# An SSD scan feeding a bilinear FFN: the first input halves, the weight transfers and the order of the first three pairs are rearranged

## The chip, the core and the metric

One core of a Trainium2 chip runs the kernel. Its five engines have queues of their own: TensorE (PE, with weight loads shown as PEld), VectorE (DVE), ScalarE (ACT), GpSimd (POOL) and SyncE (SP, which issues DMAs here and computes nothing). The metric is the device time of one execution in microseconds (us); lower is better.

## The reference

A selective state-space scan gives y; y, laid out as 3072 tokens by 256 features, goes through a bilinear feed-forward. Per batch b (4) and head h (8), over 768 positions, with a state of 16 by 32:

```python
cum = np.cumsum(la, axis=-1)                    # la = log a, within a chunk
L = np.exp(cum[:, :, :, None] - cum[:, :, None, :]) * causal
M = np.einsum('bhin,bhjn->bhij', Cc, Bc) * L
y = einsum(M, xc) + einsum(Cc, state) * exp(cum)
state = decay_full * state + sum_j(Bc xc decay_from_j)
...
a = x @ w_a; b = x @ w_b                        # x: y as 3072 x 256, d_ff = 1536
return (a * b @ w_out).astype(np.float32)
```

The chunk length is free in exact arithmetic; the kernel uses 128.

## The kernel before, in words

The sequence is cut into 6 blocks of 128 positions, and the batches into 2 couples; a *pair* p is one block of one couple (p = 2 * block + couple), so there are 12, each with 256 tokens. Rows of a pair's tiles are 64 partitions for one batch (bt = 0) and 64 for the other, two positions to a partition (index r).

For a pair the work is:

- six loads (load, L127; load1, L119): halves bt = 0, 1 of B, C and x, 64 KB each for B and C and 128 KB for x;
- scale_bc (L235) multiplies B and C by decay factors fB and fC into bm and cm, scale_x (L226) makes a 16-bit X16 of x; mostly on POOL;
- transposes (L252): four on PE, then ACT makes two copies bt and one copy ct;
- scores (L270): 32 small matmuls into the PSUM tiles SC0 and SC1;
- mask (L303), four per pair: DVE multiplies a PSUM bank by the causal mask into T1; or, "by_pool", ACT copies the bank to tmp and POOL multiplies;
- pv (L347): matmuls of the carried state (Sbd) with C and of T1 with X16, ds_mm for the state update, then ACT evacuates X2T, the transposed y; state (L380) updates the state on DVE and POOL;
- six units (unit, L409): each forms 256 of the 1536 hidden features: 8 matmuls with Wa and Wb into two PSUM banks, an ACT copy asb of the first, and a DVE product hk with the second;
- two out_half (L455): 12 matmuls of hk with Wo, an ACT copy osb and a store on SP.

The pool psf has four PSUM banks handed out in turn to the two banks of each unit, the one of each out_half, and the temporaries fps, tb, tc, py, gps. A bank is free again when its reader (asb, hk, osb, a copy) is done.

Decay factors: scan (L190) forms cumulative products Pr of a on DVE, sel_over_mid (L194) selr, and factors_mm (L203) matmuls of the two in fp32 give fC and, by a reciprocal, fB. This is done for block 0 first (8 matmuls) and for blocks 1 to 5 later (40 matmuls). hr, hs, hsx and a small matmul gps (which read the constant c32) give the decays G of the state.

The order on every engine is written out by hand: the program runs under a manual schedule, and each engine takes its instructions in the order of the source. From pair 4 on a loop (L592) repeats one pattern. Pairs 0 to 3 have a sequence of their own (L475 to L590), since the pipeline has to be filled: pair 0 is done in two halves (pv_u and evac0, u = 0, 1) so that its first unit starts early, with matmuls of zeros (warmup, L183) put between, whose results nobody reads.

DMAs are issued from three queues. SP: a, then halves of B, x, B, C, B, x, x of pairs 0 and 1, c32, then load(2), load(3) and so on. ACT: both halves of pair 0's C, half its x, half of pair 1's C. POOL: the constant ch, and the weights, which are converted to 16 bits on the way: load_w (L169) moves a third of Wa and a third of Wb (256 KB each as stored); thirds 0 and 1 early, third 2 (L498) after POOL's scaling of pair 1, then Wo (L499, 768 KB).

Of the kernel before, what the change touches and what calls it, by code (L numbers as in the profile page):

```python
# [22 lines left out]
def kernel(  # L23
# [13 lines left out]
    nc = tc.nc  # L37
# [75 lines left out]
    def tiles(p):  # L113
        Bn = inp.tile([128, H, 2, N], f32, name="bn", tag="bn")
        Cn = inp.tile([128, H, 2, N], f32, name="cn", tag="cn")
        Xn = inp.tile([128, H, 2, D], f32, name="xn", tag="xn")
        pair_in[p] = (Bn, Cn, Xn)

    def load1(eng, p, which, bt):  # L119
        blk, bp = divmod(p, NBP)  # L120
        src = (B, C, x)[which][2 * bp + bt, :, blk * Q : (blk + 1) * Q, :]
        return eng.dma_start(  # L122
            pair_in[p][which][64 * bt : 64 * bt + 64].rearrange("i h r n -> i h (r n)"),
            src.rearrange("h (i r) n -> i h (r n)", r=2),
        )

    def load(p, eng=None):  # L127
        tiles(p)
        return [load1(eng or nc.sync, p, w, bt) for w in range(3) for bt in range(2)]

    nc.sync.dma_start(a_sb, a.rearrange("b h (k q) -> (b h) k q", q=Q))
    tiles(0)
    tiles(1)
    load1(nc.scalar, 0, 1, 1)
    load1(nc.sync, 0, 0, 0)
    load1(nc.scalar, 0, 1, 0)
    load1(nc.sync, 0, 0, 1)
    nc.scalar.preload_act_table_set("natural_log_exp_and_others")
    load1(nc.scalar, 0, 2, 1)
    load1(nc.sync, 0, 2, 0)  # L140
    load1(nc.scalar, 1, 1, 1)
    load1(nc.sync, 1, 0, 0)
# [1 line left out]
    load1(nc.sync, 1, 0, 1)  # L144
    load1(nc.sync, 1, 2, 0)
    load1(nc.sync, 1, 2, 1)
    nc.sync.dma_start(c32, p32_t.ap())
    load(2)
    nc.vector.memset(warm.bitcast(u32), 0)
    nc.vector.memset(zero, 0.0)  # L150
# [18 lines left out]
    def load_w(q3):  # L169
        for W, src in ((Wa, moe_w_a), (Wb, moe_w_b)):  # L170
            c = slice(q3 * KC, (q3 + 1) * KC)
            wd.append(nc.gpsimd.dma_start(W[:, :, c], src.rearrange("(f p) e -> p f e", p=128)[:, :, c]))
# [3 lines left out]
    for bt in range(2):  # L176
# [2 lines left out]
            out=v, in_=v, compare_op=ALU.is_ge, fill=0.0, base=0, pattern=[[-1, 2], [1, Q]], channel_multiplier=-2  # L179
        )  # L180
    load_w(1)

    def warmup(n, bank, cols=512):  # L183
        for _ in range(n):
            nc.tensor.matmul(
                bank[:, 0:cols], warm[:, 0:128], warm[:, 0:cols], start=True, stop=True, skip_group_check=True
            )
# [32 lines left out]
    def flat(f, lo, hi):  # L220
        return f[:, lo:hi].rearrange("p k r b h -> p (k r b h)")
# [4 lines left out]
    def scale_x(p, eng):  # L226
        X16 = mid.tile([128, H, 2, D], f16, name="x16", tag="x16")
        xo, xi = X16.rearrange("p h r d -> p (h r d)"), pair_in[p][2].rearrange("p h r d -> p (h r d)")
        st.setdefault(p, {})["X16"] = X16
        if eng is nc.scalar:  # L230
            nc.scalar.mul(xo, xi, XS)  # L231
        else:
            eng.tensor_scalar(xo, xi, XS, None, ALU.mult)  # L233

    def scale_bc(p, which, eng):  # L235
        blk, bp = divmod(p, NBP)
        name, f = (("bm", fB), ("cm", fC))[which]
        m_ = mid.tile([128, 2, H, N], f16, name=name, tag=name)
        eng.tensor_tensor(  # L239
            out=m_,  # L240
            in0=pair_in[p][which].rearrange("p h r n -> p r h n"),
            in1=f[:, blk, :, bp].unsqueeze(3).broadcast_to((128, 2, H, N)),
            op=ALU.mult,
        )
        st.setdefault(p, {})[name] = m_
# [6 lines left out]
    def transposes(p, ps=None):  # L252
        s = st[p]
        TB, TC = (TT[:, 0:256], TT[:, 256:512]) if ps is None else [t_.bitcast(f16)[:, 0:256] for t_ in ps]
        for T_, src in ((TB, s["bm"]), (TC, s["cm"])):
            for r in range(2):
                nc.tensor.transpose(  # L257
                    T_[:, r * 128 : (r + 1) * 128], src[:, r].rearrange("p h n -> p (h n)"), ident
                )
        BT = mid.tile([128, 2, 2, 2, 64], f16, name="bt", tag="bt")  # L260
        CT = mid.tile([128, 2, Q], f16, name="ct", tag="ct")
        for e in range(2):
            o_ = BT[:, e].rearrange("p r t i -> p (r t i)")
            nc.scalar.activation(out=o_, in_=TB, func=AF.Copy, scale=par[:, e : e + 1])  # L264
        (nc.scalar.copy if ps is None else nc.vector.tensor_copy)(
            CT.rearrange("p t (i r) -> p r (t i)", r=2), TC.rearrange("p (r c) -> p r c", r=2)
        )
        s["BT"], s["CT"] = BT, CT

    def scores(p):  # L270
        BT, CT = st[p]["BT"], st[p]["CT"]
        for e in range(2):
            for r in range(2):
                for m in range(4):
                    for bt in range(2):
                        rows = slice(32 * m, 32 * m + 32)
                        c0 = (e * 2 + r) * Q
                        nc.tensor.matmul(  # L278
                            SC[m][64 * bt : 64 * bt + 64, c0 : c0 + Q],
                            BT[rows, e, r, bt],  # L280
                            CT[rows, bt],
                            start=True,
                            stop=True,
                            skip_group_check=True,
                            tile_position=(32 * m, 64 * bt),
                        )
        st[p]["T1"] = mid.tile([128, H, 2, Q], f16, name="t1", tag="t1")

    def product(p, m):

        return (
            st[p]["T1"][:, 2 * m : 2 * m + 2].rearrange("p e r q -> p e (r q)"),
            SC[m].rearrange("p (e c) -> p e c", e=2),
        )

    def product0(m2, e):

        return (
            st[0]["T1"][:, 4 * m2 : 4 * m2 + 4].rearrange("p (m e) r q -> p e m (r q)", e=2)[:, e],
            (SC0, SC1)[m2][:, :, e * 256 : e * 256 + 256],  # L300
        )

    def mask(out_in, by_pool=False):  # L303
        o_, i_ = out_in
        c_ = causal.rearrange("p r q -> p (r q)").unsqueeze(1).broadcast_to((128, 2, 2 * Q))
        if by_pool:
            tmp = mid.tile([128, 2, 2 * Q], f32, name="tmp", tag="tmp")
            nc.scalar.copy(tmp, i_)  # L308
            nc.gpsimd.tensor_tensor(out=o_, in0=tmp, in1=c_, op=ALU.mult)  # L309
        else:  # L310
            nc.vector.tensor_tensor(out=o_, in0=i_, in1=c_, op=ALU.mult)  # L311
# [149 lines left out]
    def bank(name):  # L461
        return psf.tile([128, 512], f32, name=name, tag="ff")

    def fb(k):
        nc.vector.reciprocal(flat(fB, k, k + 1), flat(fC, k, k + 1))

    def go(*items):
        for p, k2 in items:
            unit(p, k2)()
# [2 lines left out]
        if ("S", p) in st:  # L472
            st[p].update(st.pop(("S", p)))

    warmup(7, SC[3])  # L475
    scan(0, 1)
    sel_over_mid(0, 1)
    v = factors_mm(0, 1)
# [9 lines left out]
    scan(2, 3)  # L488
    warmup(1, SC[3])
    scores(0)  # L490
    scale_x(0, nc.scalar)
    mask(product0(0, 0))
    mask(product0(0, 1))
    mask(product0(1, 1), by_pool=True)
    mask(product0(1, 0))
    scale_bc(1, 1, nc.gpsimd)
    scale_bc(1, 0, nc.gpsimd)
    load_w(2)  # L498
    nc.gpsimd.dma_start(Wo, moe_w_out.rearrange("(k p) e -> p k e", p=128))  # L499
    nc.gpsimd.tensor_copy(maskbd, headm.unsqueeze(2).broadcast_to((128, H, D)))  # L500
    load(3)
    warmup(3, tcp)
    py = [bank("py0"), bank("py1")]
    pv_u(0, 0, py, True)
# [3 lines left out]
    pv_u(0, 1, py, True)  # L508
    for bt in range(2):
        evac0(1, bt, (nc.scalar, nc.vector)[bt], py)  # L510
    warmup(2, tcp)
    scan(3, NBLK)
    h = unit(0, 0)
    sel_over_mid(1, NBLK)
    h()
    go((0, 1))
    transposes(1)
    nc.vector.tensor_tensor(out=hr, in0=Pr[:, 0:NG, Q - 1], in1=rmid[:, 0:NG], op=ALU.mult)
    nc.vector.tensor_tensor(out=hs, in0=hr, in1=Pr[:, 1:NBLK, 63], op=ALU.mult)
# [3 lines left out]
        in1=selb.rearrange("p (b g) -> p b g", b=nb),  # L523
        op=ALU.mult,
    )
    v = factors_mm(1, NBLK)
    nc.scalar.copy(flat(fC, 1, NBLK), v)
    scores(1)
    fb(1)
    mask(product(1, 3), by_pool=True)  # L530
    scale_x(1, nc.scalar)
    mask(product(1, 2))
    mask(product(1, 0))
    h = unit(0, 2)
    mask(product(1, 1))
    h()
    h = unit(0, 3)
    gps = bank("gps")
    nc.tensor.matmul(
        gps[:, 0 : nb * NG], indm, hsx.rearrange("p b g -> p (b g)"), start=True, stop=True, skip_group_check=True  # L540
    )
    nc.scalar.copy(G.rearrange("p b g -> p (b g)"), gps[:, 0 : nb * NG])
    h()
    scale_bc(2, 1, nc.gpsimd)
    scale_bc(2, 0, nc.gpsimd)
    ds_mm(0, 320)
    pv(1)
    state(0)
    state(1)
    go((1, 0), (1, 1))  # L550
    transposes(2)
    go((1, 2), (1, 3))
    scores(2)
    mask(product(2, 3), by_pool=True)
    mask(product(2, 0))
    h = unit(0, 4)
    mask(product(2, 1))
    h()
    mask(product(2, 2), by_pool=True)
    go((0, 5), (1, 4), (1, 5))  # L560
    scale_x(2, nc.scalar)
    scale(3)
    pull(2)
    pv(2)
    state(2)
    fb(2)
    load(4)
    out_half(0, 0)
    transposes(3)
    out_half(0, 1)  # L570
    go((2, 0))
    scores(3)
    scale(4)
    load(5)
    h = unit(2, 1)
    mask(product(3, 0))
    h()
    mask(product(3, 1))
    out_half(1, 0)
    mask(product(3, 2))  # L580
    h = unit(2, 2)
    mask(product(3, 3))
    h()
    out_half(1, 1)
    go((2, 3))
    pull(3)
    pv(3)
    state(3)
# [71 lines left out]
```

## Time and profile before

| | |
|---|---|
| five runs, median (lowest to highest) | 133.95 us (132.63 to 133.97) |
| the profiled execution, its own time | 133.61 us |
| its span, first to last instruction | 131.9 us |
| PE busy (matmuls) | 122.6 us, 93% of the span |
| PE weight loads | 101.5 us, 77% |
| DVE busy | 86.2 us, 65% |
| ACT busy | 75.4 us, 57% |
| POOL busy | 53.9 us, 41% |
| moved by DMA | 12.22 MB, mean 93 GB/s |

The page of a profile gives for each engine its busy time and, below, the span in 40 slices of 3.3 us with the busy tenths of each. PEclk is the share of full clock that TensorE was granted. The chain of waits follows the last instruction back to what released it, step by step. The windows view gives busy time by stretch. "L311" is line 311 of the kernel before; lines shift by a few in the changed kernel.

### The profile page before, as it was taken

What the parts mean: (1) busy time and instruction counts of PE and PEld (TensorE: products, weight loads), DVE (VectorE), ACT (ScalarE), POOL (GpSimd) and SP (SyncE); (2) the same over time, 40 slices, a digit from 0 to 9 for tenths busy, and PEclk for the clock granted to TensorE, in tenths of its full rate; (3) what the DMA queues carried; (4) which work ended last, traced back from release to release, by engine and by line L of the source; (5) the groups of instructions that cost most, each with busy time, mean ns of one, the idle gap of its engine ahead of it and who ended that gap; (6) DMA issues with size and microseconds to landing.
All of it is one profiled execution on the core that took longest, in us unless ns stands there. A gap on an engine that the chain in (4) does not pass through costs nothing.

```text
span 131.9 us, 4722 instructions
## 1 busy us (share of the span) xinstructions
PE 122.6 (93%) x1947; PEld 101.5 (77%) x1947; DVE 86.2 (65%) x162; ACT 75.4 (57%) x155; POOL 53.9 (41%) x73
## 2 busy tenths in 40 slices
PE   6867997988999999999999999999999999999980
PEld 2324877867888788888888888888898888888870
DVE  2576677784483994974975956957939929744440
ACT  3162575965637738547566476476575485465420
POOL 7914885596901916607409309129047000000000
PEclk9997799999999999999999999999999999999998
DMA  3999899944348521541542443614511110110102
GB/s 69 176 197 214 112 190 220 211 77 102 95 73 194 98 73 45 84 117 45 85 119 59 65 124 72 120 53 89 110 50 40 33 51 5 40 40 5 50 30 80
DMA packets 44805, 12.22 MB, mean 93 GB/s; under 512 B 38576, under 2 KB 44752, under 8 KB 44784
## 3 DMA queue, kind: packets, MB, share of 16 engines
q1 hardware_dynamic: 39312, 9.10, 33.3%
q0 software_dynamic: 3216, 2.36, 12.2%
q10 hardware_dynamic: 2256, 0.46, 1.8%
q8 instruction: 15, 0.25, 0.8%
q14 instruction: 6, 0.05, 0.2%
HBM read 11.13 MB, written 3.15 MB: 108 GB/s over the span
## 4 chain that ended last, share of the span: by engine, by line
PE 81%; DMA 4%; DVE 4%; ACT 3%; issue 2%; SPq 1%; POOL 1%; ACTq 0%; POOLq 0%
PE ops L436 24%; PE aps L419 23%; PE bps L419 22%; DMA xn<-in_x_dram 4%; PE SC L320 3%; PE SC L278 3%; PE SC L257 2%; DVE t L311 2%; DVE hk L429 2%; PE SC L354 2%; PE SC L337 1%; SPq L122 1%; PE fps L209 1%; ACT x L231 1%; POOL t L309 1%
## 5 line engine op out<-in xcount | busy, mean ns | idle before, releaser
L429 DVE TENSOR_TENSOR hk<-bps,asb 128x512 f16<-128x512 f32 x72 | 49.1, 688 | 28.1 <-ACT asb L428 25.5
L428 ACT COPY asb<-aps 128x512 f32<-128x512 f32 x72 | 41.9, 587 | 19.8 <-PE aps L419 17.3
L419 PE MATMUL aps<-X2T,Wa 128*128 128x256 f16 x288 | 44.2, 277 | 0.7 <-ACT X2T L366 0.7
L419 PE MATMUL bps<-X2T,Wb 128*128 128x256 f16 x288 | 44.1, 277 | 0.5 <-DVE hk L429 0.4
L436 PE MATMUL ops<-Wo,hk 128*128 128x256 f16 x288 | 35.2, 273 | 0.0
L419 PEld LDWEIGHTS <-Wb 128*128 128x128 f16 x288 | 28.6, 99 | 4.5 <-issue 0.8
L419 PEld LDWEIGHTS <-Wa 128*128 128x128 f16 x288 | 27.4, 99 | 5.3 <-issue 0.7
L436 PEld LDWEIGHTS <-hk 128*128 128x128 f16 x288 | 27.7, 98 | 3.2
L311 DVE TENSOR_TENSOR t<-SC,causal 128x512 f16<-128x512 f32 x44 | 28.8, 682 | 1.1 <-ACT tmp L308 0.8
L394 POOL TENSOR_TENSOR sbd<-U,maskbd 128x512 f16<-128x512 f32 x10 | 11.6, 1158 | 38.7 <-DVE U L390 37.2
L451 ACT ACTIVATE osb<-ops 128x256 f32<-128x256 f32 x23 | 8.8, 383 | 18.0 <-PE ops L436 17.9
L233 POOL TENSOR_SCALAR x<-xn 128x512 f16<-128x512 f32 x9 | 13.4, 1489 | 0.8
L366 ACT ACTIVATE X2T<-SC 128x512 f16<-128x512 f32 x11 | 6.6, 597 | 7.0 <-PE SC L337 6.0
L264 ACT ACTIVATE bt<-SC,ch 128x256 f16<-128x256 f16 x22 | 9.2, 471 | 0.5 <-PE SC L257 0.5
L239 POOL TENSOR_TENSOR bm<-bn,fB 128x256 f16<-128x256 f32 x11 | 6.8, 621 | 1.6 <-DVE selr L196 1.6
L390 DVE SCALAR_TENSOR_TENSOR U<-SC,G,gU 128x64 f32<-128x64 f32 x16 | 3.8, 279 | 5.4 <-ACT X2T L366 5.4
L239 POOL TENSOR_TENSOR cm<-cn,fC 128x256 f16<-128x256 f32 x11 | 6.8, 620 | 0.6 <-DMA cn<-in_C_dram 0.6
L320 PEld LDWEIGHTS <-x 64*32 64x32 f16 x384 | 3.2, 91 | 4.5 <-ACT x L231 1.9
L309 POOL TENSOR_TENSOR t<-tmp,causal 128x512 f16<-128x512 f32 x4 | 4.6, 1154 | 4.8 <-ACT tmp L308 4.8
L320 PE MATMUL SC<-t,x 64*32 64x128 f16 x352 | 4.8, 219 | 0.8 <-ACT x L231 0.5
L278 PEld LDWEIGHTS <-bt 32*64 32x64 f16 x384 | 3.4, 104 | 2.7 <-issue 1.9
L278 PE MATMUL SC<-ct,bt 32*64 32x128 f16 x384 | 5.1, 220 | 0.3 <-ACT bt L264 0.3
(59 smaller groups left out, 70.4 us busy)
## 6 DMA issues: line engine op xcount, KB each, us to landing
xn<-in_x_dram SPq DMA_DIRECT2D x23, 128.0 KB, 3.4
out_dram<-osb SPq DMA_DIRECT2D x23, 128.0 KB, 1.7
bn<-in_B_dram SPq DMA_DIRECT2D x24, 64.0 KB, 3.3
cn<-in_C_dram SPq DMA_DIRECT2D x21, 64.0 KB, 3.3
Wa<-in_moe_w_a_dram POOLq DMA_DIRECT2D x3, 256.0 KB, 5.4
Wb<-in_moe_w_b_dram POOLq DMA_DIRECT2D x3, 256.0 KB, 6.5
Wo<-in_moe_w_out_dram POOLq DMA_DIRECT2D x1, 768.0 KB, 10.8
cn<-in_C_dram ACTq DMA_DIRECT2D x3, 64.0 KB, 3.6
```

The lines of the kernel that those rows point to most:

```text
L233: eng.tensor_scalar(xo, xi, XS, None, ALU.mult)
L239: eng.tensor_tensor(out=m_, in0=pair_in[p][which].rearrange("p h r n -> p r h n"), in1=f[:, blk, :, bp].unsqueeze(3).broadcast_to((128, 2, ...
L264: nc.scalar.activation(out=o_, in_=TB, func=AF.Copy, scale=par[:, e : e + 1])
L278: nc.tensor.matmul(SC[m][64 * bt : 64 * bt + 64, c0 : c0 + Q], BT[rows, e, r, bt], CT[rows, bt], start=True, stop=True, skip_group_check=True,
L311: nc.vector.tensor_tensor(out=o_, in0=i_, in1=c_, op=ALU.mult)
L320: nc.tensor.matmul(py[bt][32 * g : 32 * g + 32, u * Q : (u + 1) * Q], s["X16"][k, h, r, :], s["T1"][k, h, r, :], start=(first and u == 0 a ...
L394: nc.gpsimd.tensor_tensor(out=Sbd.rearrange("p t (m c) -> p t m c", m=4), in0=U32[:, p].unsqueeze(2).broadcast_to((128, 2, 4, 2 * D)), in1 ...
L419: nc.tensor.matmul(ps[:, kk * 2 * Q : (kk + 1) * 2 * Q], W[:, f, k * 128 : (k + 1) * 128], X2T[:, p, f].rearrange("p t q -> p (t q)"), sta ...
L428: nc.scalar.copy(asb, a_ps)
L429: return lambda: nc.vector.tensor_tensor(out=s["hk"][:, 2 * k2 : 2 * k2 + 2, :].rearrange("p k q -> p (k q)"), in0=b_ps, in1=asb, op=ALU.mult)
L436: nc.tensor.matmul(o_ps[:, 0:d_model], hk[:, k, bt * Q : (bt + 1) * Q], Wo[:, k, :], start=(k == 0), stop=(k == NK - 1), skip_group_check= ...
L451: nc.scalar.activation(out=o_sb, in_=o_ps[:, 0:d_model], func=AF.Copy, scale=1.0 / (YS * YS))
```

## The change

All work stays but for fewer columns of warm-up; what moves is order, queue and two DMA waits.

- Pair 0's loads: ACT issues half of B first, then half of C; SP the other half of B, then of C. (Before: both halves of B on SP, both of C on ACT.) The constant c32 goes from SP to ACT.
- The third weight transfer (Wa, third 1) waits until ACT's half of pair 0's x has landed. Third 2 of Wa and Wb is issued ahead of POOL's scaling of pair 1. Pair 3's first load waits until Wo has landed.
- Warm-ups: 7 of 512 columns become 6 and one of 128; ahead of unit(0,0) 2 become 1 and one of 128.
- Pair 0's mask by POOL comes ahead of scale_x(0) on ACT.
- The later decay products (40 matmuls and the copy fC) come ahead of transposes(1).
- unit(0,2) comes ahead of scores(1), unit(0,4) ahead of pv(1), unit(0,5) right after it; hk and asb of these are put between pair 1's masks.
- scores(2) come behind (0,5) and (1,0) to (1,4), five units of pair 1; pair 2's third mask goes from POOL to DVE; scale_x(2) moves ahead of the last asb of pair 1.
- out_half(0,0) comes ahead of pv(2); of pair 2, unit(2,1) comes ahead of scores(3).

```diff
+    load1(nc.scalar, 0, 0, 1)
+    load1(nc.sync, 0, 0, 0)
     load1(nc.scalar, 0, 1, 1)
-    load1(nc.sync, 0, 0, 0)
-    load1(nc.scalar, 0, 1, 0)
-    load1(nc.sync, 0, 0, 1)
+    load1(nc.sync, 0, 1, 0)
     nc.scalar.preload_act_table_set("natural_log_exp_and_others")
-    load1(nc.scalar, 0, 2, 1)
+    x_in = load1(nc.scalar, 0, 2, 1)
+    nc.scalar.dma_start(c32, p32_t.ap())
...
-    nc.sync.dma_start(c32, p32_t.ap())
...
+    tc.add_manual_dep(wd[2].ins, x_in.ins.name, AFTER, reason="inputs first")
...
-    warmup(7, SC[3])
+    warmup(6, SC[3])
+    warmup(1, SC[3], 128)
...
+    mask(product0(1, 1), by_pool=True)
     scale_x(0, nc.scalar)
     mask(product0(0, 0))
     mask(product0(0, 1))
-    mask(product0(1, 1), by_pool=True)
     mask(product0(1, 0))
+    load_w(2)
     scale_bc(1, 1, nc.gpsimd)
     scale_bc(1, 0, nc.gpsimd)
-    load_w(2)
-    nc.gpsimd.dma_start(Wo, moe_w_out.rearrange("(k p) e -> p k e", p=128))
+    wo_d = nc.gpsimd.dma_start(Wo, moe_w_out.rearrange("(k p) e -> p k e", p=128))
...
-    load(3)
+    n0 = load(3)
+    tc.add_manual_dep(n0[0].ins, wo_d.ins.name, AFTER, reason="weights first")
...
-    warmup(2, tcp)
+    warmup(1, tcp)
+    warmup(1, tcp, 128)
...
     go((0, 1))
+    v = factors_mm(1, NBLK)
+    nc.scalar.copy(flat(fC, 1, NBLK), v)
     transposes(1)
...
-    v = factors_mm(1, NBLK)
-    nc.scalar.copy(flat(fC, 1, NBLK), v)
+    h = unit(0, 2)
+    fb(1)
     scores(1)
-    fb(1)
     mask(product(1, 3), by_pool=True)
-    scale_x(1, nc.scalar)
     mask(product(1, 2))
-    mask(product(1, 0))
-    h = unit(0, 2)
-    mask(product(1, 1))
     h()
     h = unit(0, 3)
+    mask(product(1, 0))
+    scale_x(1, nc.scalar)
     gps = bank("gps")
...
+    mask(product(1, 1))
     h()
...
+    go((0, 4))
     ds_mm(0, 320)
     pv(1)
     state(0)
     state(1)
-    go((1, 0), (1, 1))
+    go((0, 5), (1, 0), (1, 1), (1, 2))
     transposes(2)
-    go((1, 2), (1, 3))
+    go((1, 3))
+    h = unit(1, 4)
     scores(2)
     mask(product(2, 3), by_pool=True)
+    h()
+    scale_x(2, nc.scalar)
     mask(product(2, 0))
-    h = unit(0, 4)
+    h = unit(1, 5)
     mask(product(2, 1))
+    mask(product(2, 2))
     h()
-    mask(product(2, 2), by_pool=True)
-    go((0, 5), (1, 4), (1, 5))
-    scale_x(2, nc.scalar)
+    out_half(0, 0)
     scale(3)
     pull(2)
     pv(2)
...
-    out_half(0, 0)
+    out_half(0, 1)
     transposes(3)
-    out_half(0, 1)
-    go((2, 0))
+    go((2, 0), (2, 1))
     scores(3)
...
-    h = unit(2, 1)
+    h = unit(2, 2)
     mask(product(3, 0))
...
-    h = unit(2, 2)
+    h = unit(2, 3)
     mask(product(3, 3))
     h()
     out_half(1, 1)
-    go((2, 3))
```

add_manual_dep(later, earlier) makes the first DMA's issue wait for the second's landing.

## The prediction

> **What bounds the kernel now.** I read the page first: the busy rows by slice, then the granted clock and the DMA row under them.
>
> ```profile
> PE   6867997988999999999999999999999999999980
> ...
> PEclk9997799999999999999999999999999999999998
> DMA  3999899944348521541542443614511110110102
> ```
>
> A slice is 3.3 us. From slice 10 on TensorE (PE) is full. What is left to gain lies in the first nine slices: there PE has holes, its clock falls to 7 tenths in slices 3 and 4, and DMA is at 9. The same by stage, from the windows view (columns: stretch, length, busy PE, PEld, DVE, ACT, POOL, then clock, DMA share, GB/s):
>
> ```profile
> 8.10:11.50 3.40, 1.85 (x37) 0.72 (x36) 1.85 (x4) 1.82 (x5) 1.21 (x2) 1.00 1.32 205
> 11.50:15.00 3.50, 3.50 (x19) 2.41 (x18) 2.59 (x7) 1.17 (x2) 1.90 (x4) 0.51 1.10 187
> 15.00:20.20 5.20, 4.95 (x159) 4.13 (x158) 3.90 (x10) 3.71 (x9) 4.46 (x6) 1.00 1.04 158
> 20.20:20.90 0.70, 0.00 (x1) 0.03 (x1) 0.61 (x2) 0.60 (x1) 0.00 (x0) 1.00 1.43 211
> 20.90:30.70 9.80, 8.79 (x153) 7.40 (x153) 7.21 (x14) 7.03 (x14) 7.64 (x9) 1.00 1.12 155
> 41.00:131.90 90.90, 87.21 (x1360) 75.42 (x1359) 60.72 (x107) 53.23 (x108) 28.42 (x33) 1.00 0.29 68
> ```
>
> The last row holds no hole but the drain at the end (41 to 128: 86.97 of 87.00 busy). The change doesn't touch that loop, so every microsecond won must come from reaching unit(2,0), which starts at 33.49, earlier. The chain of waits says what stands before it (start, length, what):
>
> ```profile
> 2.65 5.71 DMA xn<-in_x_dram
> 8.38 0.63 ACT x L231
> 9.01 0.48 ACT tmp L308
> 9.65 1.16 POOL t L309
> ...
> 14.21 0.85 PE bps L419 x4
> ...
> 16.63 0.46 PE SC L278 x32
> 17.11 0.59 ACT tmp L308
> ...
> 20.28 0.61 ACT X2T L366
> ...
> 27.15 0.69 DVE hk L429
> 27.89 0.60 PE bps L419 x4
> ...
> 29.44 0.64 ACT x L231
> 30.13 0.42 PE SC L320 x32
> ```
>
> So there are five losses: pair 0's second half waits for the masking on GpSimd (POOL), behind ACT's tmp, behind x; units at half clock (4 matmuls in 0.85 us, later 0.44); the X2T of pair 1 (PE idle 20.2 to 20.93); a PSUM bank that a late hk holds (0.61 before 27.89); and x of pair 2, scaled late (0.63 before 30.13).
>
> **What the skill says.** (1) TensorE: Matmul & The Clock Gate, Part 1 (HAM clock gate): the clock is halved unless activity in windows of 3413 ns holds it open. The trace agrees: a thin stretch of 3.4 us (1.85 busy), then 0.51 for 3.5 us. The threshold isn't stated. (2) DMA: Bandwidth & Descriptors, Queues, rings and completion order: each engine alternates between the queues that have work, by packet. The trace agrees in kind; in 5 to 13 us the weights (q0) and SP's loads (q1) show
>
> ```profile
> q0 software_dynamic: 1080, 1.04, 80.4%
> q1 hardware_dynamic: 2656, 0.46, 37.9%
> ```
>
> or 332 SP packets per us, against 1993 in the 2 us from 13, when the weights have stopped. (3) The same page, Issuing engines are not separate DMA queues: moving a DMA from SP to ACT saves issue time only.
>
> **The change, part by part.** Times are those of the profiled execution (span 131.9 us, 133.61 in all; the median of the runs shown, 133.95, is 0.34 above it).
>
> *Pair 0's inputs and warm-ups.* Six and a quarter warm-ups instead of seven take 0.32 off ahead of the decay products (cold pitch 0.43 times three quarters): they start at 4.02 rather than 4.34, selr being done at 3.83. fB ends at 5.01. B's second half moves from SP's second B slot (issued 1.99, landing 3.5 later) to ACT's first (0.79), where C's landed at 3.5; so bm starts at 5.05, not 5.57. C's half takes the 1.99 slot and lands at 5.45: cm starts at 5.57, not 5.92. Hence scores(0) 0.34 earlier, at 6.87. c32's issue moves to ACT, waits there for B's half (3.5) and takes some 0.6; behind it stand C of pair 1 and the fC copy, due at 5.05: ready 4.75, so no cost (if the issue took the 1.52 that it took on SP, cm would be 0.6 late). SP loses that issue and keeps its other order. X itself doesn't move: landed 8.36, X16 at 9.01, first pv_u at 9.07 as before.
>
> *Tmp ahead of x.* ACT copies tmp at 7.44 to 8.01, in the time in which it waited for x; POOL masks 8.17 to 9.32 (it ended at 10.80); DVE's third mask no longer waits until 9.52 and ends at 9.35. The second pv_u can start at 9.6 instead of 10.85, its evacuation ends at 10.25, and unit(0,0) runs from 10.3 instead of 11.66: 1.35 us. Two warm-ups became one and a quarter, inside this.
>
> *Clock.* The thin stretch now gets some 1.3 us of dense units before 11.6. I take it that the clock stays open: a unit costs 0.875, not 1.70. The bound on the other side comes below.
>
> *Weights.* The third weight transfer now waits for half of x (landing 6.2); behind it on POOL are the fourth's issue (to 7.7) and the mask at 8.17: 0.5 slack, and the queue still has the second in flight until 10.0, so nothing is lost. The last two are issued at about 9.4 and 10.1 instead of 14.22 and 14.97. The first four landed two microseconds apart (8.2, 10.0, 12.3, 14.0): these follow at 15.9 and 17.6, in time for unit(0,4) at 18.3. POOL then scales pair 1 and issues Wo at 14.3.
>
> *Decay products ahead of transposes(1).* Units (0,0), (0,1): 10.3 to 12.05. selr comes 2.0 after the evacuation as before: 12.2. The 40 matmuls, 1.31 us: to 13.6. They now fill a wait: bm(1) needs B's half issued at 5.14 that took 8.4 us, so POOL ends at 14.3 in both kernels. PE idles 0.7, then transposes, unit(0,2), and after bt, bt, ct (1.2 us of ACT) scores(1) at 15.83, from 16.58.
>
> *Pair 1 to its X2T.* tmp 16.36 to 16.93; then DVE does mask, hk, mask, mask at some 0.64 each, to 19.5: hk(0,2) inside this row costs back 0.65, and pv(1) ends only 0.1 earlier. But PE has done unit(0,3), gps, and unit(0,4) (from 18.32, when that hk frees its bank). unit(0,5), from 20.16, covers X2T. So (1,0) starts at 21.04 against 20.93, with six units done against four: 2 x 0.875 - 0.11 = 1.64 us.
>
> *Pair 2.* From there to unit(2,0) PE has six units 5.25, two transposes 0.44, scores 0.36, pv 0.65, two out_half 2.62: 9.32, giving 30.36. Before, that and two units more, 11.07, took 12.56: 1.49 of holes, 1.24 of it the two gaps above. With scores behind five units, the masks of pair 2 end at 28.45, against PE's arrival at pv(2) at 28.2: 0.15 back. x(2) is scaled ahead of the last asb: that gap goes. The third mask leaves ACT and POOL (0.59 and 1.15) for DVE (0.65), counted above.
>
> *Loads of pairs 2 and 3.* Under weight traffic until 16 SP gets some 180 packets per us once ACT's queue is empty (10 to 12 us), then beside Wo's smaller packets some 330, then 1000: pair 2's last C half, packet 6384 of its queue, lands at about 22.5; with two POOL scalings (1.24) transposes(2) can run at 23.85, PE being there at 23.7: 0.2 back. Load(3) on SP waits until Wo has landed; Wo took 5.7 us after Wb's landing (26.5 less 20.8), so 23.3; four halves later, some 5.7 us with scaling, 29.0, against transposes(3) at 30.3: hidden, 1.3 us of cover. Behind that wait on SP stand the stores of pair 0, due from 28.6, and load(4), first needed by transposes(4) near 38 (40.9 before).
>
> Sum: 1.64 + 1.49 - 0.15 - 0.2 = 2.8; I keep 0.25 for the small holes that were there besides the two gaps, so 2.5. Profiled: 131.1; from the median 131.4. I say 131.3.
>
> **Rivals.**
> *Crowded loads (0.22).* Weights without gaps hold SP's loads back. x(1) lands at about 17 (14.8 before); from 18.9 on it delays pv(1). Pair 2 has no cover: if SP gets three quarters of the rate, C lands 1.5 later and PE stands still that long. For: DMA at 9 in slices 1 to 8. Against: 512 weight packets are all that is added before 16 us. 132.8.
> *The clock still falls at 11.6 (0.10).* Half of unit(0,1) and the decay products run slow, but 0.7 idle follows: it costs 0.3 to 0.8, so 131.6 to 132.1. For: the thin stretch is still 8.2 to 9.1 idle.
> *B of pair 1 comes earlier (0.06).* Then the 0.7 idle goes: 130.5.
> *Slower by Wo (0.05).* Load(3) hangs on one landing. Each us of Wo past 24.6 moves transposes(3) by one; slower than before from 27.2, 13 us after issue (10.8 before, when it stood behind two weights). At 29: 136. Against: its queue starts 4 us earlier.
> *Nothing moves (133.9)*: pv(1) is forecast nearly unmoved, so were DVE the bound up to unit(2,0), all would be lost again. It gets no chance of its own: DVE is busy 7.21 of 9.80 us in 20.9 to 30.7, and the two units done ahead take their hk out of that stretch.
>
> **How the numbers follow.** Forecast 0.57, its own range 130.6 to 132.0. What this kernel's measurement tells from no change is about 1%: 132.6 to 135.3. Faster: 0.57, 0.10, 0.06 and half of crowding: 0.84. Same: the other half, 0.11. Slower: 0.05. The range runs from 130.1 to 132.9, taking in the bounds on the clock and on pair 2.
>
> **What would show it.** Tmp ahead of x near 7.4; unit(0,0) at 10.3; clock 1.00 in 11.5 to 15; scores(1) at 15.8 behind a bm(1) at 13.7; pv(1) near 19.5 with unit(0,4) before it; no gap of 0.6 before pv(2); unit(2,0) at 30.8. Wrong would be: PE idle over 0.5 before transposes(2) or (3), or the clock at 0.5 after 15.

## The result, and the profile after

The changed kernel takes 132.46 us (median of 28 runs, 131.02 to 137.13) against 133.97 us for the kernel before (47 runs, 131.84 to 137.28). The ratio is 0.9941, 95% interval 0.9911 to 0.997. Here and below, medians are of all runs (these two lie 1.1% apart), but a ratio compares only the runs within 1.5% of their kernel's fastest, and leaves the slower ones out. So it is faster by 0.3 to 0.9%, where 2% was forecast; within the 1% that the prediction called the limit of what can be told from no change. The time lies inside the forecast range, at its upper part, and outside the 130.6 to 132.0 of the forecast's main case.

The profiled execution took 132.43 us, its span is 130.7 us (before: 133.61 and 131.9). Its page, the rows that answer to those shown of before:

```profile
PE   6969969698999999999999999999999999999980
...
PEclk9999999999999999999999999999999999999999
DMA  3999999263656461532533433514510110110102
```

The clock row has lost its dip. Counting slices from 1 (the prediction counts from 0), DMA is at 9 in slices 2 to 7 without a break and then falls to 2; before had an 8 in slice 5, 13 to 16 us, and went on to slice 8. PE still has holes in slices 6, 8 and 10. The windows view over the same stretches as in the prediction says how large they are:

```profile
8.10:11.50 3.40, 2.43 (x45) 1.51 (x45) 2.46 (x7) 1.64 (x5) 2.58 (x4) 1.00 1.32 208
11.50:15.00 3.50, 3.50 (x62) 2.77 (x59) 2.67 (x9) 2.01 (x6) 2.71 (x4) 1.00 1.37 207
20.90:30.70 9.80, 8.30 (x149) 6.78 (x147) 6.98 (x14) 6.18 (x13) 6.46 (x9) 1.00 0.51 91
```

The front is denser (2.43 busy, before 1.85) and the next 3.5 us hold 62 matmuls, not 19. But the stretch of pair 2, from 20.9 to 30.7, has 1.50 us without PE where before had 1.01. The chain of waits tells what TensorE stood for (start, length, what):

```profile
3.32 7.20 DMA bn<-in_B_dram
10.54 0.60 SPq L122
11.18 1.60 SPq L122
12.82 10.47 DMA cn<-in_C_dram
...
24.01 0.63 POOL bm L240
24.68 0.41 PE SC L258 x4
...
28.58 1.29 DVE t L312 x2
29.91 0.38 PE SC L355 x4
```

The chain that began in before with x of pair 0 and went on over the masks and X2T now runs through SP's queue and one DMA of 10.47 us, pair 2's last half of C. Line 258 is transposes(2), line 355 the first matmuls of pv(2). The waits view of PE from 10 to 34 us (total, times, longest) says the same:

```profile
PE SC L258 <- POOL bm L240: 1.1, 1, 1.1
PE bps L420 <- DMA Wb<-in_moe_w_b_dram: 0.9, 1, 0.9
PE SC L355 <- DVE t L312: 0.4, 1, 0.4
```

Put into stages (start of a unit's first matmul, from the timeline of PE; "pair 2" is the way from unit(1,0) to unit(2,0)):

| execution | span | unit(0,0) | unit(1,0) | unit(2,0) | pair 2 |
|---|---|---|---|---|---|
| before | 131.9 | 11.52 | 20.93 | 33.49 | 12.56, eight units |
| forecast of the change | | 10.3 | 21.04 | 31.0 (33.49 less 2.5; its list of signs says 30.8) | 9.96, six units |
| changed | 130.7 | 10.37 | 20.83 | 32.27 | 11.44, six units |

In this execution the forecast is met up to unit(1,0) and lost behind it: 1.48 us more than foreseen in pair 2. Other executions of the same order lose in another place; the section on why the prediction was wrong has them.

### The profile page after: what moved, and what is told of

Read it like the earlier page. It is cut to its first block, busy times and chain, and to the rows that moved or that the text cites. A ratio compares the mean times of both kernels' runs of the same rounds, so it can differ in the third digit from the quotient of the medians.

```text
span 130.7 us, 4718 instructions
## 1 busy us (share of the span) xinstructions
PE 121.5 (93%) x1947; PEld 100.3 (77%) x1947; DVE 86.2 (66%) x163; ACT 74.8 (57%) x154; POOL 53.2 (41%) x72
## 3 DMA queue, kind: packets, MB, share of 16 engines
q1 hardware_dynamic: 39264, 9.08, 33.1%
## 4 chain that ended last, share of the span: by engine, by line
PE 71%; DMA 14%; DVE 4%; SPq 3%; issue 3%; ACT 2%; POOL 1%; POOLq 0%; DVEq 0%
PE ops L437 23%; PE aps L420 19%; PE bps L420 19%; DMA cn<-in_C_dram 8%; DMA bn<-in_B_dram 6%; SPq L122 3%; PE SC L321 3%; PE SC L258 2%; PE SC L279 2%; PE SC L355 2%; DVE t L312 2%; DVE hk L430 2%; PE SC L338 1%; ACT asb L429 1%; ACT ct L266 1%
## 5 line engine op out<-in xcount | busy, mean ns | idle before, releaser
L430 DVE TENSOR_TENSOR hk<-bps,asb 128x512 f16<-128x512 f32 x72 | 49.0, 687 | 25.5 <-ACT asb L429 21.8
L420 PE MATMUL bps<-X2T,Wb 128*128 128x256 f16 x288 | 43.2, 273 | 1.0 <-DMA Wb<-in_moe_w_b_dram 0.9
L420 PE MATMUL aps<-X2T,Wa 128*128 128x256 f16 x288 | 43.5, 273 | 0.2
L420 PEld LDWEIGHTS <-Wb 128*128 128x128 f16 x288 | 28.0, 98 | 5.0 <-DMA Wb<-in_moe_w_b_dram 1.5
L312 DVE TENSOR_TENSOR t<-SC,causal 128x512 f16<-128x512 f32 x45 | 29.4, 681 | 2.3 <-ACT tmp L309 2.0
L420 PEld LDWEIGHTS <-Wa 128*128 128x128 f16 x288 | 26.8, 98 | 4.5 <-DVE X2T L379 0.3
L395 POOL TENSOR_TENSOR sbd<-U,maskbd 128x512 f16<-128x512 f32 x10 | 11.6, 1158 | 32.2 <-DVE U L391 32.2
L186 PE MATMUL SC<-warm 128*128 128x512 f16 (+1 forms) x11 | 4.4, 548 | 1.2 <-DVE warm L149 1.2
L266 ACT COPY ct<-SC 128x256 f16<-128x256 f16 x11 | 5.0, 455 | 0.0
```

The source lines that it names most:

```text
L395: nc.gpsimd.tensor_tensor(out=Sbd.rearrange("p t (m c) -> p t m c", m=4), in0=U32[:, p].unsqueeze(2).broadcast_to((128, 2, 4, 2 * D)), in1 ...
L420: nc.tensor.matmul(ps[:, kk * 2 * Q : (kk + 1) * 2 * Q], W[:, f, k * 128 : (k + 1) * 128], X2T[:, p, f].rearrange("p t q -> p (t q)"), sta ...
L430: return lambda: nc.vector.tensor_tensor(out=s["hk"][:, 2 * k2 : 2 * k2 + 2, :].rearrange("p k q -> p (k q)"), in0=b_ps, in1=asb, op=ALU.mult)
```

## The experiments

Kernels that ran together on one chip share their runs of the kernel before. Nothing of the reference's computation is left out in any of them. Where one time stands, the kernel ran once, for its trace, and there is no interval.

**Wo later.** Wo is issued behind pair 1's mask on POOL, and pair 3's first load doesn't wait for it.

```diff
-    wo_d = nc.gpsimd.dma_start(Wo, ...)
...
-    n0 = load(3)
-    tc.add_manual_dep(n0[0].ins, wo_d.ins.name, AFTER, reason="weights first")
+    load(3)
...
     mask(product(1, 3), by_pool=True)
+    nc.gpsimd.dma_start(Wo, ...)
```

> The changed kernel with Wo's issue moved on POOL behind the mask of pair 1 (about 17.8 us instead of 12.7), and load(3) no longer waiting for Wo. Theory A (pair 2's C halves land at 23.3 because Wo shares the DMA engines with them, and PE idles 1.1 us ahead of transposes(2), then again at pv(2)): C lands by 21.5, the wait ahead of transposes(2) goes, unit(2,0) starts at 30.8 to 31.3 instead of 32.27, span 129.3 to 129.8, ratio to the kernel before 0.980 to 0.987. Theory B (DVE's masks and products hold pv(2), whatever the loads do): transposes(2) come earlier, the idle time moves to pv(2), unit(2,0) not before 31.9, span above 130.3, ratio as for the changed kernel, about 0.994.

Measured: 132.19 us (22 runs), ratio 0.9927, interval 0.9892 to 0.9961. In its profile POOL starts cm of pair 2 at 20.13 (23.43 in the changed kernel), so C is early, as theory A says, and transposes(2) run at 24.39 directly behind unit(1,2). The waits view of PE, same stretch, has no bm any more:

```profile
PE SC L355 <- DVE t L312: 0.4, 1, 0.4
PE SC L279 <- ACT ct L266: 0.4, 1, 0.4
PE SC L321 <- DVE t L312: 0.4, 1, 0.4
```

Pair 2 takes 10.20 us instead of 11.44. But this difference isn't all due to Wo. The clock was at half from 9.08 to 12.50 here, unit(1,0) started at 21.77 (20.83 in the changed kernel), and TensorE came to transposes(2) at 24.39; scaled C of 24.63, as in the changed kernel, would have kept it for 0.24 us only. The numbers are those that theory B named: unit(2,0) at 31.97, span 130.5, ratio 0.9927. So an early C without Wo's early issue is shown; 1.2 us won is not, nor a better total, whose interval overlaps that of the changed kernel. The wait ahead of pv(2) (line 355) is there with an early C too, so it is a loss of its own.

**Transposes(2) one unit later**, behind unit(1,3), all transfers as in the changed kernel.

```diff
-    go((0, 5), (1, 0), (1, 1), (1, 2))
+    go((0, 5), (1, 0), (1, 1), (1, 2), (1, 3))
     transposes(2)
-    go((1, 3))
```

> The changed kernel with transposes(2) behind unit(1,3) instead of ahead of it; no transfer is touched. Theory A: C of pair 2 still lands at 23.3 and transposes(2) still run at 24.7, but PE has 0.87 us more to do meanwhile; scores(2) then wait some 0.5 for bt and ct, so 0.3 to 0.5 us is won: span 130.2 to 130.4. Theory B: nothing is won, since the masks come no earlier: span 130.6 to 130.8.

Measured: 132.4 us (14 runs), ratio 0.9935, interval 0.9875 to 0.9995. Pair 2 takes 10.47 us, with 0.4 before scores(2) for ct and 0.2 at pv(2); the span, 131.3, is neither theory's. C landed at 22.90 and was scaled at 24.23, late again with Wo issued at 12.67. Transposes(2) come at 25.98 without a wait, but that the extra unit covers a late C isn't shown: unit(1,0) started at 22.49 here, and TensorE would have come to transposes(2) at 25.11 without the extra unit.

**The first part alone**: the kernel before with only the new order of pair 0's inputs, the third weight transfer's wait, the warm-ups and the early tmp.

```diff
-    load1(nc.scalar, 0, 1, 0)
-    load1(nc.sync, 0, 0, 1)
+    load1(nc.scalar, 0, 0, 1)  ...
+    mask(product0(1, 1), by_pool=True)
     scale_x(0, nc.scalar)
...
-    mask(product0(1, 1), by_pool=True)
```

> The kernel before with the first part of the change alone: B halves lead, c32 on ACT, the third weight transfer behind x, the shorter warm-ups, pair 0's POOL mask ahead of x. Theory A: the first unit starts at 10.4 as in the changed kernel, transposes(1) at some 12.8, pv(1) by 18, and pair 2's loads are as early as before (16.4), so unit(2,0) starts at 31.2 to 32.0 and the span is 129.6 to 130.4: as fast as the whole change or faster. Theory C (the later order of units is what gains, the front alone is given back in pair 1's masks): unit(2,0) at 33 or later, span 131.3 to 131.9.

Measured: 132.47 us (22 runs), ratio 0.9958, interval 0.9925 to 0.9991. It keeps before's waits (0.7 for X2T just ahead of pair 2; 0.5 for x and 0.4 for the hk bank in it) and pair 2 takes 12.55 us; the span, 131.3, is theory C's, and unit(2,0), at 32.92, nearly so. Yet its median, measured apart, is that of the whole change (132.47 and 132.46), and the intervals overlap. So what the later parts add to the total can't be told from nothing here.

**Six warm-ups more** in the kernel before, three ahead of each half of pair 0's pv, to see what the dense stretch does to the clock.

```diff
-    warmup(3, tcp)
+    warmup(6, tcp)
...
-    warmup(1, tcp)
+    warmup(4, tcp)
```

> The kernel before with six more warm-up matmuls of 512 columns in the thin stretch from 8 to 11 us, where PE waits anyway. Theory D (the half clock is worth its full price, 1.7 us): clock 1.00 in 11.5 to 15, span 130.2 to 130.5. Theory A (B of pair 1 lands at 13.5 and would hold transposes(1) at 14.3 anyway, 14.86 before): clock 1.00, but only 0.4 to 0.6 won, span 131.2 to 131.5.

Measured: 133.73 us (14 runs), ratio 0.9998, interval 0.993 to 1.0066. Inconclusive: the clock opened only at 10.26 us in its profile, the warm-ups ran at half rate and held the first pv_u up to 10.59 (9.07 in before) and the second to 11.80.

**Third 2 of the weights at its old place**, behind POOL's scaling of pair 1, and **the third weight transfer without its wait for x**; each ran once.

```diff
-    load_w(2)
     scale_bc(1, 1, nc.gpsimd)
     scale_bc(1, 0, nc.gpsimd)
+    load_w(2)
```

> The changed kernel with the weights' third 2 back behind POOL's scaling of pair 1 (issued at about 12.7 instead of 9.35). Theory Q (POOL's queue still holds the second third until 14.5, so that the issue time moves nothing): third 2 of Wb lands at 18.3 to 19.2 (18.7 in the changed kernel), pair 2's last C at 22.8 to 23.8, the wait ahead of transposes(2) 0.8 to 1.4. Theory G (issuing without gaps is what crowds SP's loads): C lands 1 us or more earlier and that wait falls under 0.4.

```diff
-    tc.add_manual_dep(wd[2].ins, x_in.ins.name, AFTER, reason="inputs first")
```

> The changed kernel without the wait of the third weight transfer for half of x. Theory I (that wait is why B of pair 1 lands at 11.6 instead of 13.5): B lands at 13 or later, POOL's bm of pair 1 is at 13.2 or later, transposes(1) 0.3 or more later. Theory J (the wait moves nothing, as I forecast): B lands at 11.3 to 12.3 as in the changed kernel.

Measured: 132.72 and 132.67 us. In the first, Wo goes out at 14.20 and POOL has pair 2's C at 20.73, as theory G says; in the second, B of pair 1 came late (landed 14.51, bm(1) at 14.63), as theory I says, Wo went out at 15.20, and POOL starts cm of pair 2 at 19.63 without having waited for it. TensorE came to transposes(2) at about 25 in both and didn't wait. Their pair 2 took 10.20 us each.

**A held start.** So that the clock would be open in every run, 22 warm-ups come first and all other queues wait for them; the four kernels are before, the changed one, Wo later, and Wo later with a split out_half (below).

```diff
+    for _ in range(22):
+        hold = nc.tensor.matmul(SC[3][:, 0:512], warm[:, 0:128], warm, ...)
...
+    for f_ in first:
+        tc.add_manual_dep(f_.ins, hold.ins.name, AFTER, reason="hold")
```

> The kernel before, held open: 22 matmuls of zeros come first and every other queue waits for them, and the later warm-ups are more (14, 4, 2, 6, 3, 2), so that TensorE is dense from the start; all times from the release on are to be read against the other held kernels, and the whole is 7 to 9 us longer. Theory D' (the clock opens and shuts at a phase that differs from run to run, and that makes most of the spread and much of the difference): the clock is open from the release on, the runs spread less, and unit(2,0) starts at the release plus 32.0 to 32.3. Theory A says the same of this kernel; it is the baseline.

> The changed kernel, held open in the same way (14, 4, 2, 6, 1, 1 and a quarter). Theory D' (what the change wins is mostly that units meet no half clock, and its order is worth little by itself): 0.3 to 0.8 us less than the kernel before held open. My forecast's order terms (two units ahead of pair 1, two gaps gone): 2 us or more less.

> The changed kernel with Wo's issue behind pair 1's POOL mask and load(3) free, held open. Theory A (Wo beside pair 2's loads costs the wait ahead of transposes(2)): 0.9 to 1.3 us less than the changed kernel held open. Theory B (DVE holds pv(2) anyway): 0 to 0.4 less.

> As the last, and half of out_half(0,1) comes ahead of pv(2), the other half behind it. Theory A with the vector order as the second cost: PE's 0.4 to 0.6 ahead of pv(2) is filled, 0.4 to 0.6 us less than the last. If pair 3's or Wo's loads are the next bound, nothing.

Measured: 141.38, 140.78, 141.99 and 141.2 us (medians of 6 runs each). As a way to compare totals this failed: in 17 of the 24 runs the mean granted clock is 0.988 or less (the two of the four profiles with such a mean show a shut stretch of 3.41 us), and x of pair 0 landed anywhere from 14.69 to 18.75 in the profiles. What can be used are the stages: pair 2 takes 12.56, 11.24, 10.48 (0.86 of it a wait for Wo) and 10.03 us, and the changed kernel waits 1.0 ahead of transposes(2) here too.

**Wo later, with load(3) still behind it, and out_half(0,1) split round pv(2)**:

```diff
     mask(product(1, 3), by_pool=True)
+    wo_d = nc.gpsimd.dma_start(Wo, ...)
+    n0 = load(3)
+    tc.add_manual_dep(n0[0].ins, wo_d.ins.name, AFTER, reason="weights first")
```

The lines of Wo and load(3) at the old place go. The split is shown at the last kernel of this section.

> The changed kernel with Wo issued behind pair 1's POOL mask, load(3) still behind Wo's landing, and out_half(0,1) in two halves, one ahead of pv(2) and one behind. Theory A: from unit(1,0) to unit(2,0) PE takes 9.6 to 10.0 us (11.44 in the changed kernel, 10.20 with Wo later alone, and 9.32 is the matmul work), since Wo now lands by 25.5, pair 2's loads have the engines first and the gap ahead of pv(2) is filled; 0.9 to 1.6 us less than the changed kernel's median. Rival: load(3) behind a later Wo holds transposes(3), a new wait of 0.5 or more, and the median is as with Wo later alone.

Measured: 136.46 us (6 runs), ratio 1.0301, interval 1.0209 to 1.0392. Wo was issued at 19.49 and landed at 29.16; only then did pair 3's loads start. The waits of PE from 10 to 36:

```profile
PE SC L258 <- POOL bm L240: 2.6, 1, 2.6
PE ops L437 <- DMA Wo<-in_moe_w_out_dram: 0.9, 1, 0.9
```

The 2.6 are transposes(3). Theory A's Wo "by 25.5" was missed by 3.7 us. The kernel was meant to be faster; it became the prediction's slower rival instead, which gave 136 for a landing at 29.

**Before once more**, for the spread of its profile.

> The kernel before once more, for a second execution's trace. Theory D' (the clock opens and shuts at a phase that differs from run to run): the first opening is at another time than 4.8 us and the half clock lies elsewhere or is missing; from unit(1,0) to unit(2,0) PE takes 12.5 to 12.6 us as in the first trace, and what differs in the span lies before unit(1,0).

Measured: 133.02 us, span 131.3. unit(1,0) at 20.38 and unit(2,0) at 32.94, each 0.55 earlier than in the profile that the prediction was made from; pair 2 again 12.56. The windows view shows where the 0.55 is from:

```profile
11.50:15.00 3.50, 2.94 (x32) 2.04 (x34) 3.28 (x9) 1.65 (x4) 2.21 (x3) 1.00 1.05 180
```

Granted clock 1.00, where the first profile has 0.51: the same kernel, the same stretch, no dip. With the clock open, TensorE waits 0.6 us ahead of transposes(1) for the scaled B of pair 1, which landed at 13.41, so the open clock brings only the 0.55.

**The last four**, on one chip: Wo later with out_half(0,1) split and load(3) free; the changed kernel without pair 3's wait only; the changed kernel once more; and, first, the kernel before with the weights' early issue only:

```diff
+    load_w(2)
+    nc.gpsimd.dma_start(Wo, ...)
     scale_bc(1, 1, nc.gpsimd)
     scale_bc(1, 0, nc.gpsimd)
-    load_w(2)
-    nc.gpsimd.dma_start(Wo, ...)
```

> The kernel before with one thing changed: the third weight transfers and Wo are issued ahead of POOL's scaling of pair 1, so Wo's at about 12.3 instead of 15.69. Theory (Wo issued early takes the rate from pair 2's loads): C of pair 2 lands after 22.5 (before: by 18.9), and TensorE, which comes to transposes(2) at about 22.7, stands there 1 to 2.5 us; unit(1,0) to unit(2,0) takes 13.5 to 15 us instead of 12.56; time 135 to 136.5. Rival (the lateness in the changed kernel comes from its new order of pair 0's inputs or its loads of pair 1): C lands by 20, no wait over 0.3, 134 to 134.5 for the later scaling of pair 1 alone.

Measured: 135.31 us (4 runs), ratio 1.0216, interval 1.0103 to 1.0329; pair 2 takes 13.83 us. Wo went out at 11.92. Waits and chain of this kernel (the two waits are transposes(1), 1.2, and transposes(2), 1.1):

```profile
PE SC L257 <- POOL bm L239: 2.3, 2, 1.2
```

```profile
13.48 9.75 DMA cn<-in_C_dram
...
23.94 0.63 POOL bm L239
24.61 0.41 PE SC L257 x4
```

Nothing else of the change is in this kernel, and the same DMA lands as late as in the changed one (23.23 against 23.30), with the same wait of TensorE ahead of transposes(2). The early issue alone does it, and without the rest of the change it costs 1 to 3%; 1.27 us of that are in pair 2 (13.83 less 12.56), the rest lies elsewhere and isn't taken apart.

The changed kernel without pair 3's wait, and the changed kernel as it is:

```diff
-    n0 = load(3)
-    tc.add_manual_dep(n0[0].ins, wo_d.ins.name, AFTER, reason="weights first")
+    load(3)
```

> The changed kernel without pair 3's wait for Wo; Wo's issue stays at its early place. Theory (Wo's packets hold back pair 2's loads): the wait on pair 3 is without effect there; pair 2's last half of C still lands near 23, TensorE stands 1 to 1.5 us ahead of transposes(2), and unit(1,0) to unit(2,0) takes 11.3 to 11.7 us; 132.3 to 132.6. Rival (the wait itself holds SP's queue up): the stretch falls to 10.2 and C lands by 20.5.

> The changed kernel once more. If the wait ahead of transposes(2) belongs to the order of the transfers, it is there again, 0.9 to 1.4 us, with Wo issued within 0.3 us of 12.7 and C's half landed within 0.5 us of 23.3. If it belonged to one execution, it is below 0.5.

Measured: 132.67 us (20 runs), ratio 0.9985, interval 0.9949 to 1.0022, span 131.2; and 133.0 us, span 131.3. C of pair 2 landed at 23.49 and 22.95, as expected of Wo's early issue: pair 3's wait is innocent. But TensorE did not stand ahead of transposes(2) and pair 2 took 10.20 us in both, against what I had expected. By the second expectation's own test, the late C belongs to the order of the transfers, and the wait for it to one execution. TensorE came to transposes(2) only at 25.28 and 25.32: in the first its clock opened at 14.08 only; in the second it waited 1.4 us for selr ahead of the 40 decay products, and the clock shut from 16.50 to 19.91. The wait for selr is one of DVE's three scans, which took 1.77 us where the same scan took 0.39 in the changed kernel's first profile; POOL's two scalings of pair 1 (11.52 to 12.72) ran beside it. The start of transposes(2) is the later of two: TensorE's arrival, and the scaled C, at 24.3 to 24.8 in these traces. A good execution of the front wins nothing beyond that.

Wo later with the split, load(3) free; beside the edit of Wo later:

```diff
+    o01 = bank("ops")
+    out_mm(0, 1, o01, range(NK // 2))
     pv(2)
...
-    out_half(0, 1)
+    out_mm(0, 1, o01, range(NK // 2, NK))
+    out_store(0, 1, o01)
```

> The changed kernel with Wo issued behind pair 1's mask on POOL, pair 3's first load free of Wo, and out_half(0,1) cut in two: its first half of matmuls ahead of pv(2), its second behind. Theory: the two waits of pair 2 that were seen (1.1 ahead of transposes(2), 0.4 to 0.6 ahead of pv(2)) are all that is left there, so from the start of unit(1,0) to that of unit(2,0) it takes 9.7 to 9.9 us (11.44 in the changed kernel, 10.20 without Wo's crowding), and the time is 131.4 to 131.9, a ratio of 0.985 to 0.99. Rival: the wait ahead of pv(2) only moves behind it (X2T or pair 3's copies come late): 10.2 us again and 132.2.

Measured: 132.54 us (22 runs), ratio 0.9982, interval 0.9939 to 1.0024. Pair 2 takes 9.89 us (expected 9.7 to 9.9): the timeline of PE has pv(2) directly behind 18 matmuls of out_half.

```profile
28.89 2.14 PE L437 MATMUL ops<-Wo,hk 128*128 128x256 f16 x18
30.86 0.39 PE L355 MATMUL SC<-ct,sbd 128*128 128x128 f16 x4
```

The second wait is a loss of its own, and 0.31 us of it comes back. The total that I expected (131.4 to 131.9) was missed all the same: the span is 130.9, with the clock at half from 11.21 to 14.62. A version better than the changed kernel isn't shown.

## Why the prediction was wrong, point by point

The profile shown above comes first; other executions follow below. *Front: right here.* Decay products at 4.02 and unit(0,0) at 10.37 (10.3 forecast); POOL's mask 8.24. *B of pair 1* landed at 11.64, not 13.5: the forecast carried its 8.4 us over from before. So there is no idle before transposes(1), and scores(1) start at 15.40, not 15.83. The forecast held that the third weight transfer's wait for x moves nothing; without that wait B landed at 14.51 (one execution). *Weights:* issued at 9.35 and 10.11 as forecast, but landed at 17.2 and 18.72 (15.9 and 17.6): unit(0,4)'s second half waits 0.9 for Wb. The two errors nearly cancel and leave unit(1,0) at 20.83, forecast 21.04: that it is so close is luck.

*Loads of pairs 2 and 3: this is the step that failed.* "Pair 2's last C half ... lands at about 22.5; ... transposes(2) can run at 23.85, PE being there at 23.7: 0.2 back." Measured: landed 23.30, POOL's two scalings to 24.63, transposes(2) at 24.68, PE there at 23.46: 1.22 back. The mechanism stood in the text and among the rivals ("Pair 2 has no cover"); its size was 1.0 short. What was mis-sized is not SP's rate, which was higher than forecast. The forecast counts SP's packets as one row and lets the DMA land with "packet 6384 of its queue", at 22.5. In the trace the 6384th packet of SP's queue started at 20.61 already; but the landing is told in sixteen parts, of which thirteen were in by 20.50, fifteen by 21.98 and the last at 23.30. With the last part at 21.98 too, C would have been scaled by about 23.3 (an estimate: 1.33 from landing to the end of the scalings, as here), ahead of TensorE. In before the same sixteen lay between 15.57 and 16.38. The forecast put this lag of the last part at nothing; why it was so long is open. Nor was the load's price in the kernel before read to the end. The DMA view of 12 to 17 us, before and then changed (queue, packets, MB, share of 16 engines; the weights are q0, SP's loads q1):

```profile
q1 hardware_dynamic: 3082, 0.50, 59.8%
q0 software_dynamic: 198, 0.19, 33.2%
```

```profile
q0 software_dynamic: 789, 0.72, 91.7%
q1 hardware_dynamic: 1834, 0.30, 44.9%
```

Before, the fourth weight transfer landed at 14.0, the fifth was issued at 14.22, and only 198 weight packets moved in these 5 us: SP's queue had the larger part of the engines' time (59.8% against 33.2%) and drained, 3082 packets. The gap in the weights that the change closes was what pair 2's loads were using. That engines share by packet between queues, as the Trainium skill says (DMA: Bandwidth & Descriptors, Queues, rings and completion order), agrees in kind with these counts, and in before from 22 to 24 us, beside Wo, each queue moved 657 packets; the shares over a longer stretch had to be measured. Over the executions (POOL starts cm of pair 2 when the last C half is there and POOL is free; packets are those of POOL's and of SP's queue from 13 to 18 us, by the DMA view):

| execution | Wo issued | POOL's, SP's packets | cm of pair 2 | wait ahead of transposes(2) |
|---|---|---|---|---|
| before, Wo early | 11.92 | 967, 1702 | 23.36 | 1.26 |
| changed again | 12.66 | 1000, 1783 | 23.08 | 0, PE came at 25.32 |
| transposes(2) later | 12.67 | 1079, 1395 | 23.04 | 0, PE came at 25.98 |
| changed | 12.71 | 967, 1812 | 23.43 | 1.22 |
| load(3) free | 13.82 | 960, 1464 | 23.62 | 0, PE came at 25.28 |
| third 2 at old place | 14.20 | 550, 2393 | 20.73 | 0 |
| no wait for x | 15.20 | 672, 2389 | 19.63 or earlier | 0 |
| before | 15.69 | 254, 2580 | 18.90 or earlier | 0 |
| Wo later | 19.02 | 559, 2719 | 20.13 or earlier | 0 |

The jump between 13.82 and 14.20 is not one of Wo's time alone (the kernel at 14.20 also has third 2 later). It goes with the packets: where POOL's queue moved 960 or more in these 5 us, C came late; where it moved 672 or fewer, whether by a pause ahead of third 2 or ahead of Wo, SP's queue moved 2389 or more and C came early. No kernel changes this pause alone.

*Pair 2's masks.* "The masks of pair 2 end at 28.45, against PE's arrival at pv(2) at 28.2: 0.15 back." They ended at 29.86 and PE arrived at 29.31: 0.60 back by the timeline. It isn't only a follower of the late C: Wo later has the same 0.4 in its waits, and the split takes it away. The two terms, 1.02 and 0.45 more than forecast, are the 1.48 us that pair 2 lacks.

*Other executions.* The same order, up to transposes(2), ran in three more traces:

| execution | unit(0,0) | unit(1,0) | C scaled | unit(2,0) |
|---|---|---|---|---|
| forecast | 10.3 | 21.04 | 23.85 | 31.0 |
| changed | 10.37 | 20.83 | 24.63 | 32.27 |
| changed again | 10.95 | 22.69 | 24.28 | 32.90 |
| load(3) free | 11.60 | 22.66 | 24.82 | 32.86 |
| transposes(2) later | 11.10 | 22.49 | 24.23 | 32.96 |

In the last three the loss comes before unit(1,0), 1.45 to 1.65 us against the forecast, and the late C costs nothing. What failed there is "I take it that the clock stays open": it shut from 16.50 to 19.91, opened at 14.08 only, and shut from 10.84 to 14.26. In the first of the three the unforeseen wait for selr comes on top. The rival on the clock had put its price at 0.3 to 0.8; how much of the loss is the clock's isn't taken apart. So the front's good match above is one execution's, and the forecast needed both: an open clock and an early C.

*The clock.* "I take it that the clock stays open": it did in the first profile. There, what failed is the other side: the half clock of before from 11.6 to 15 was taken as a property of that kernel. Before again, with an open clock, is 0.55 earlier at unit(1,0). Against that execution the change brings 20.38 to 20.83 with two units more (1.75 - 0.45 = 1.30) and loses 0.63 in pair 2 (10.81 of before's way with six units, 11.44 now): 0.67 net, 131.3 to 130.7 in span. Against the first profile it is 1.2.

*Slower by Wo:* right in mechanism and in place, shown by its own kernel; the changed one has Wo landing at 23.12 (23.3 forecast, by two errors that cancel: Wb landed 1.1 later, and Wo 4.4 behind it, not 5.7), so it doesn't decide. *x of pair 2, the hk bank, X2T of pair 1:* all three gaps went, as forecast.

What stays open: how much of the ratio 0.9941 is the change and how much the mix of clocks in the runs. Among the runs of before made beside the experiments, the 51 with a mean granted clock of at least 0.994 have the median 132.55, 62 with 0.978 to 0.994 have 134.30; of the changed kernel's first 28 runs, 20 have 132.36 and 6 have 132.64. That would be a gain of 0.2 at one clock and of 1.7 at the other, and a fixed time for transposes(2) would give just such a picture; but the mean hides when the clock shut, and the runs are from several chips, so this is argued and not shown.

## What to carry to other kernels

Before a gap in one DMA queue is closed, look at which other queue drains in it, and at the first reader of what lands there: rate that one queue leaves can be what the next stage lives on. A transfer has landed when its last part has: read how far that part lags, and don't take a queue's packet count for a landing. A stretch that is won in front of a landing is only won up to that landing, so work out its time first and put the cover (units that need nothing new) in front of it. Take a second profile of the kernel before, and of the changed one: what differs between two executions of one kernel can't be counted on as a gain, and a wait seen in one may be missing in the next.

## What was not expected of the hardware

The clock's dips have no fixed place. In these profiles the clock first opened at 4.76 us in before and 5.57 in before again, 5.81 and 9.67 in the changed kernel and its repeat, 14.08 in load(3) free; then it shut for 3.41 us at 11.59 in before, 16.50 in the repeat, and not at all in others. The Trainium skill says so of the windows (TensorE: Matmul & The Clock Gate, Part 1: free-running, so that the count of cold matmuls differs from run to run) and calls the penalty of this first ramp under 1% of a typical span. The groups above, whose means hold the later dips too, lie 1.3% apart for before (134.30 over 132.55).

And the clock column reads 1.00 before the first opening although the array runs at half rate. The timeline of PE in load(3) free, whose windows view gives 1.00 throughout:

```profile
12.46 1.06 PE L420 MATMUL bps<-X2T,Wb 128*128 128x256 f16 x4
...
16.64 0.60 PE L420 MATMUL bps<-X2T,Wb 128*128 128x256 f16 x4
```

The same four matmuls take 1.06 us at 12.46 and 0.60 at 16.64; the clock opened in between, at 14.08, and the column doesn't move. Early in a span the length of the matmuls has to be read, not the column.

DVE's scans of 32x128 take 0.38 to 0.42 us wherever no computing instruction of POOL overlaps them, in all the traces shown here. Every scan that took longer, 0.43 to 0.84 us and once 1.77, had POOL computing beside it; some that POOL overlapped took no longer. That POOL holds them up is argued from this, not tested.
